# Reordering the first two chunks of a chunked DeltaNet with SwiGLU: copies by pairs of batches, K turned earlier, a chain spread over four gate/value pairs

## The chip, the cores and the metric

The kernel runs on one core of a Trainium2 chip. The metric is device time in microseconds (us). Executions of one kernel on one chip are compared in the same rounds with executions of the kernel before. In the traces PE is TensorE, DVE VectorE, ACT ScalarE and POOL GpSimd. The granted clock is the share of TensorE's full clock that a trace records; "warm" stands for 1.00 and "cold" for 0.50. PSUM is the memory that the matmuls of this kernel write; `ps_pair` gives out two of its banks by a tag.

A ratio is the mean time of one kernel's fast runs over the mean time of the other's fast runs of the same rounds, so it is not quite the ratio of the medians that stand beside it. Below 1 means faster than the kernel before. The interval behind it is a 95% interval.

## The reference, cut to what matters

```python
# q, k, v: (4, 8, 768, 48) float32, beta: (4, 8, 768)
k_n = k / (np.linalg.norm(k, axis=-1, keepdims=True) + 1e-06)
for t in range(S):                                  # S = 768, per batch and head
    y[:, :, t] = np.einsum('bhd,bhde->bhe', q[:, :, t], state)
    v_old = np.einsum('bhde,bhd->bhe', state, kt)
    state = state + bt * np.einsum('bhd,bhe->bhde', kt, vt - v_old)
x = y.transpose(0, 2, 1, 3).reshape(B * S, H * D)   # (3072, 384)
g = x @ w_gate                                      # (384, 1536)
out = (g / (1 + np.exp(-g)) * (x @ w_val)) @ w_out  # (1536, 384)
```

The kernel does this in 12 chunks of 64 time steps. Within a chunk the recurrence becomes products with the inverse of a triangular matrix. VectorE makes these inverses by substitution, for two chunks at a time (a group): the first inverse serves chunks 0 and 1, the second 2 and 3, the third 4 and 5. One chunk then goes through four steps, `p_r`/`p_y` (state times K and Q), `p_u` (inverse times V), `p_s`/`p_y` (new state, output) and `p_f` (transposes of y), and after that through the feed-forward block: six pairs of `p_gate`/`p_val` and two outputs `p_o`, each long enough to keep TensorE full.

## The kernel before

The order of TensorE's work is written out by hand. `point(c)` puts one step of chunk `c`, or one preparation, between two pairs; `prep_step` picks the preparation:

```python
    def prep_step(c):
        if first:
            first.pop(0)()
            return True
        # ... joins of finished inverses ...
        if going:
            next(going.pop())
            return True
        if not q_of or steps("advance", q_of[0] - 1) < 3:
            return False
        k_c, q_c = None, q_of.pop(0)
        if k_of and steps("advance", k_of[0] - AHEAD) >= 4:   # AHEAD = 4
            k_c = k_of.pop(0)
        # ... K of chunk k_c and Q of chunk q_c are turned; an odd k_c also starts an inverse ...
```

The last part of `advance(c)`, the chain of a chunk, with its two copies out of PSUM:

```python
        p_y = recur(ps_pair("p_y", "py"))
        # ...
        p_of_u()
        y = work.tile([128, NB, NJ, 2, D], FP32, name="y", tag="r", bufs=3)
        nc.scalar.copy(y[:, :, :, 0], p_y[:, 0])
        for b in range(2):
            nc.scalar.copy(y[half_of(b), :, :, 1], p_y[half_of(1 - b), 1])
        yield
        p_f = ps_pair("p_f", "py")[:, :, 0 : KT * 128]
        # ... six transposes of y into p_f ...
        nc.scalar.copy(xts[c].rearrange("p t (bp n) -> p t bp n", bp=NB), p_f)
        if c == 0:
            of_state()
        yield
```

And an inverse begins with transposes on VectorE, then a power on GpSimd, then VectorE again:

```python
    def invert(g):
        # ... three transposes into mb (VectorE) ...
        nc.gpsimd.tensor_tensor(out=n, in0=mb[...], in1=half, op=ALU.pow)
        yield WAIT
        nc.vector.tensor_scalar_add(n, n, 1e-6)        # waits for the power
        # ... reciprocal, scaling, 31 substitution steps ...
```

## Time and profile before

| | us |
|---|---|
| median of the three runs that the prediction had | 792.59 (791.41 to 794.15) |
| the execution that was profiled | 788.7, span 786.7, mean granted clock 0.964 |
| TensorE busy | 737.0 of 786.7 |
| TensorE's idle time after 209.5 us | 6.1 |

The prediction shows the lines that bound this kernel. Four more marks of its TensorE timeline serve as a measure (start, length, engine, line, operation, shapes, count): the first `p_o` ends the twelve pairs of chunks 0 and 1, `p_j` is the join of the second inverse, then come chunk 2's `p_u` and its first gate.

```profile
155.44 20.80 PE L754 MATMUL p_o<-wo_sb,h_f 128*128 128x384 f32 x64
182.44 1.92 PE L502 MATMUL p_j<-zt,a_sb 32*32 32x32 f32 x64 [6.20 <-issue]
199.91 1.15 PE L654 MATMUL p_u<-vin,zt 64*64 64x48 f32 x64
209.45 2.86 PE L731 MATMUL p_gate<-x_ffn,wg_sb 128*128 128x256 f32 x12
```

### The profile page before, as it was taken

How to read it: one execution, taken by the hardware profiler on the slowest of the kernel's cores; microseconds unless marked ns; L12 is line 12 of the kernel's file. 1: busy time of each engine (PE TensorE's matmuls, PEld its weight loads, DVE VectorE, ACT ScalarE, POOL GpSimd, SP SyncE). 2: the span in 40 equal slices, each digit the busy share in tenths (PEclk: the TensorE clock that was granted, in tenths of full speed). 3: DMA queues.
4: the chain of work that ended last, by engine and by line, in shares of the span. 5: the costliest groups of instructions: out<-in, count | busy, mean ns of one | idle time of the engine just before them, and what ended most of it. 6: DMA issues, size and time to landing. Idle time of an engine off the chain costs nothing.

```text
span 786.7 us, 21538 instructions
## 1 busy us (share of the span) xinstructions
PE 737.0 (94%) x9800; PEld 588.2 (75%) x9800; DVE 403.8 (51%) x814; ACT 163.6 (21%) x296; POOL 67.9 (9%) x52
## 2 busy tenths in 40 slices
PE   5638899997999999999999999999999999999997
PEld 4537788855788688688688688688688688687784
DVE  5999699994127873067842068832068822021010
ACT  2246243201221211212111112111212111111110
POOL 9106000100003000012000021000020000000000
PEclk9856899998999999999999999999999999999999
DMA  8874244200211200312101112101101000000000
GB/s 149 205 189 116 88 108 137 61 20 12 53 22 23 45 17 3 61 23 42 32 12 19 39 28 43 31 13 23 26 17 22 21 2 2 21 2 1 21 1 20
DMA packets 86683, 34.77 MB, mean 44 GB/s; under 512 B 78848, under 2 KB 81920, under 8 KB 86592
## 3 DMA queue, kind: packets, MB, share of 16 engines
q1 hardware_dynamic: 79872, 27.93, 15.8%
q10 hardware_dynamic: 5952, 5.12, 2.9%
q8 instruction: 77, 1.26, 0.7%
q0 software_dynamic: 768, 0.35, 0.3%
q14 instruction: 14, 0.11, 0.0%
HBM read 28.66 MB, written 4.72 MB: 42 GB/s over the span
## 4 chain that ended last, share of the span: by engine, by line
PE 89%; DVE 5%; ACT 1%; issue 1%; POOL 1%; DMA 1%; ACTq 0%; DVEq 0%
PE p_gate L731 25%; PE p_o L754 24%; PE p_val L731 24%; PE p_g L389 3%; PE p_t L377 2%; PE p_j L517 2%; PE p_u L654 2%; PE p_s L683 2%; PE p_y L671 2%; DVE zb L459 1%; DVE tmp L453 1%; PE p_r L633 1%; PE p_y L642 1%; PE p_f L714 1%; POOL n_t L319 1%
## 5 line engine op out<-in xcount | busy, mean ns | idle before, releaser
L731 PE MATMUL p_gate<-x_ffn,wg_sb 128*128 128x256 f32 x864 | 203.9, 386 | 0.0
L731 PE MATMUL p_val<-x_ffn,wv_sb 128*128 128x256 f32 x864 | 199.3, 381 | 0.0
L754 PE MATMUL p_o<-wo_sb,h_f 128*128 128x384 f32 x576 | 192.4, 491 | 0.0
L731 PEld LDWEIGHTS p_val<-x_ffn,wv_sb 128*128 128x128 f32 x864 | 164.7, 191 | 22.4
L745 DVE TENSOR_TENSOR h_f<-sil,p_val 128x512 f32<-128x512 f32 x72 | 49.3, 685 | 257.1 <-PE p_val L731 256.6
L731 PEld LDWEIGHTS p_gate<-x_ffn,wg_sb 128*128 128x128 f32 x864 | 161.2, 191 | 23.0
L754 PEld LDWEIGHTS p_o<-wo_sb,h_f 128*128 128x128 f32 x576 | 108.7, 192 | 71.8 <-issue 1.4
L740 ACT ACTIVATE sil<-p_gate 128x512 f32<-128x512 f32 x72 | 43.0, 597 | 217.4 <-PE p_gate L731 188.4
L544 POOL TENSOR_TENSOR n_b<-mb,half 128x32 f32<-128x32 f32 x5 | 39.4, 7874 | 441.0 <-DVE mb L423 403.1
L459 DVE TENSOR_TENSOR zb<-zb,tmp 128x31 f32<-128x31 f32 (+15 forms) x186 | 63.7, 343 | 6.4
L453 DVE TENSOR_TENSOR tmp<-zb,mb 128x31 f32<-128x31 f32 (+15 forms) x186 | 63.6, 342 | 5.6
L762 ACT COPY o_sb<-p_o 128x384 f32<-128x384 f32 x24 | 11.5, 478 | 172.0 <-PE p_o L754 165.5
L208 ACT ACTIVATE h_f<-h_f,rebias 128x256 int32<-128x256 uint32 (+2 forms) x36 | 21.0, 612 | 47.0 <-DVE h_f L200 47.0
L692 DVE TENSOR_TENSOR state<-state,p_s 128x768 f32<-128x768 f32 x10 | 9.5, 951 | 26.1 <-PE p_s L683 26.1
L377 PE MATMUL p_t<-ident,kn 128*128 128x128 f32 x96 | 16.8, 324 | 6.5 <-DMA kn<-in_k_dram 5.7
L502 PE MATMUL p_j<-zt,a_sb 32*32 32x32 f32 x256 | 6.2, 214 | 17.3 <-DVE zt L486 11.1
L423 DVE STREAM_TRANSPOSE mb<-a_sb 32x1024 f32<-32x1024 f32 x10 | 21.3, 2135 | 0.3
L377 PEld LDWEIGHTS p_t<-ident,kn 128*128 128x128 f32 x96 | 13.3, 166 | 9.8 <-POOL mask_q L273 4.5
L402 DVE TENSOR_TENSOR p_sb<-p_g,mask_q 128x512 f32<-128x512 f32 x24 | 15.4, 684 | 8.4 <-PE p_g L389 8.4
L389 PEld LDWEIGHTS p_g<-kt 64*64 64x64 f32 x768 | 13.9, 149 | 7.7 <-issue 4.2
L502 PEld LDWEIGHTS p_j<-zt,a_sb 32*32 32x32 f32 x256 | 5.8, 129 | 18.5 <-issue 18.4
L389 PE MATMUL p_g<-kt 64*64 64x64 f32 x768 | 15.5, 236 | 3.7 <-ACT kt L379 2.3
(120 smaller groups left out, 583.9 us busy)
## 6 DMA issues: line engine op xcount, KB each, us to landing
qpad<-in_q_dram SPq DMA_DIRECT2D x48, 96.0 KB, 3.0
vin<-in_v_dram SPq DMA_DIRECT2D x96, 48.0 KB, 2.5
out_dram<-o_sb ACTq DMA_DIRECT2D x48, 96.0 KB, 2.2
kn<-in_k_dram SPq DMA_DIRECT2D x44, 96.0 KB, 3.7
zt<-in_moe_w_out_dram SPq DMA_DIRECT2D x6, 384.0 KB, 3.1
staged<-in_moe_w_out_dram SPq DMA_DIRECT2D x6, 384.0 KB, 3.1
wo_sb<-in_moe_w_gate_dram SPq DMA_DIRECT2D x4, 512.0 KB, 5.5
wo_sb<-in_moe_w_val_dram SPq DMA_DIRECT2D x4, 512.0 KB, 6.9
```

What stands on the lines that cost most here:

```text
L208: nc.scalar.activation(power.bitcast(I32), power, ACTF.Relu, bias=rebias, scale=8.0)
L377: nc.tensor.transpose(p_t[bp][:, at], x[:, bp, 2 * j : 2 * j + 2], ident)
L389: nc.tensor.matmul(p_v[par][half_of(b if of_q else b ^ par), bp, j], kt[c][half_of(par), bp, j, b], xt[half_of(par), bp, j, b],)
L423: nc.vector.transpose(out(rows, 0), in_(rows, 0))
L453: nc.vector.tensor_tensor(out=t_v, in0=zb[:, 0 : j + 1, j : j + 1].to_broadcast([128, j + 1, m]), in1=mb[:, j : j + 1, j + 1 : R].to_broad ...
L459: nc.vector.tensor_tensor(out=zb[:, 0 : j + 1, j + 1 : R], in0=zb[:, 0 : j + 1, j + 1 : R], in1=t_v, op=ALU.add,)
L517: nc.tensor.matmul(p_j[h // n_h][hi, h % n_h, 0:R] if of_d else p_j[h // n_h][hi, h % n_h, R:C], d_t[hi, :, HH * c + h], ident[hi, hi] if ...
L544: nc.gpsimd.tensor_tensor(out=n, in0=mb.rearrange("p j i -> p (j i)")[:, 0 : R * R : R + 1], in1=half, op=ALU.pow,)
L731: nc.tensor.matmul(ps[name][:, i], w_sb[:, t, (f + i) * 128 : (f + i + 1) * 128], xts[c][:, t], start=(t == 0), stop=(t == KT - 1),)
L740: nc.scalar.activation(sil, ps[name], ACTF.Silu)
L745: nc.vector.tensor_tensor(out=hs[c, f], in0=sil, in1=ps["p_val"], op=ALU.mult)
L754: nc.tensor.matmul(p_o, hs[c, f - f % 2][:, f % 2, bp * 128 : (bp + 1) * 128], wo_sb[:, f], start=(f == 0), stop=(f == FT - 1),)
```

## The change

Its intent is to give TensorE work earlier and to fill its waits: shorter copies in chunk 0's chain, so that the first gate starts sooner; chunk 1's chain between four pairs of chunk 0 instead of three; K of chunk 5 in the idle time during chunk 0's outputs. The diff, cut to its core:

```diff
-        nc.scalar.copy(uu, p_u)
+        each = range(NB) if c == 0 else (slice(0, NB),)
+        for bp in each:
+            nc.scalar.copy(uu[:, :, bp], p_u[:, :, bp])
@@ y by pairs of batches; zt and x_ffn likewise
+        for bp in each:
+            nc.scalar.copy(y[:, bp, :, 0], p_y[:, 0, bp])
+            for b in range(2):
+                nc.scalar.copy(y[half_of(b), bp, :, 1], p_y[half_of(1 - b), 1, bp])
@@ prep_step: a K alone may be taken
-        if not q_of or steps("advance", q_of[0] - 1) < 3:
+        k_c, q_c = None, None
+        if q_of and steps("advance", q_of[0] - 1) >= 3:
+            q_c = q_of.pop(0)
+        elif not (hold and k_of and steps("advance", k_of[0] - AHEAD) >= 4):
             return False
-        k_c, q_c = None, q_of.pop(0)
@@ start: K of chunk 1 turned before gram 0, the reciprocal before the transposes
         turned(0, False)
+        turned(1, False, "py")
         gram(0, False)
-        turned(1, False, "py")
+        r_b = first_n()
@@ p_s and the join of chunk 1 go into the first pair
-        next(second)
+        def state_and_join():
+            step("advance", advance, 0)
+            next(second)
-        first.append(second_join)
+        first.extend((state_and_join, second_join, lambda: gram(1, True)))
-        pairs = [(0, 0), (0, 2), (0, 4)] + [(1, 0), (1, 2), (1, 4)]
-        pairs += [(c, f) for f in range(6, FT, 2) for c in range(2)]
+        pairs = [(c, f) for c in range(2) for f in range(0, 8, 2)]
+        pairs += [(c, f) for f in range(8, FT, 2) for c in range(2)]
```

Left out here are the order of the beta loads and of the first transposes of Q, and one `point(2)` fewer ahead of chunk 1's outputs.

More of the change, by code (lines that the diff above doesn't have):

```diff
@@ L336, in load_beta, with first_n @@
         )
-    def first_betas():
+    def first_n():
         n = n_t[0].rearrange("p c h -> p (c h)")
@@ L344, in first_betas @@
         nc.vector.transpose(r_b, r_n)
-        divide_beta(0, r_b)
+        return r_b
     def scale_v_heads(c):
@@ L465, in substitute, with recur @@
             yield
+    def recur(p, m=D):
+        p = p[:, :, 0 : NB * NJ * m]
+        return p.rearrange("p x (bp j d) -> p x bp j d", bp=NB, j=NJ)
     QUADS = [(slice(R * n, R * n + R), R * (n % 2)) for n in range(4)]
@@ L510, in join_late @@
         yield
-        p_j = [p.rearrange("p (h i) -> p h i", i=C) for p in banks("p_j", tags[1])]
-        n_h = HH // 2
+        p_j = recur(ps_pair("p_j", tags[1]), C)
         for of_d in (True, False):
             for h in range(HH):
+                par, bp, j = h // (NB * NJ), h // NJ % NB, h % NJ
                 for s in range(2):
@@ L517, in join_late @@
                     nc.tensor.matmul(
-                        p_j[h // n_h][hi, h % n_h, 0:R] if of_d
-                        else p_j[h // n_h][hi, h % n_h, R:C],
+                        p_j[hi, par, bp, j, 0:R] if of_d else p_j[hi, par, bp, j, R:C],
                         d_t[hi, :, HH * c + h],
@@ L522, in join_late @@
                     )
+        zt_v = zt[:, c].rearrange("p (par bp j) i -> p par bp j i", par=2, bp=NB)
         copies = nc.scalar.copy, nc.vector.tensor_copy if split else nc.scalar.copy
-        for s, copy in enumerate(copies):
-            hi = QUADS[2 * s][0]
-            for n in range(2):
-                copy(zt[hi, c, n * n_h : (n + 1) * n_h], p_j[n][hi])
+        for bp in range(NB):
+            for s, copy in enumerate(copies):
+                hi = QUADS[2 * s][0]
+                copy(
+                    zt_v[hi, :, bp].rearrange("p par j i -> p par (j i)"),
+                    p_j[hi, :, bp].rearrange("p par j i -> p par (j i)"),
+                )
         yield
@@ L616, in join @@
         yield
-    def recur(p):
-        return p[:, :, 0 : NB * NJ * D].rearrange("p x (bp j d) -> p x bp j d", bp=NB, j=NJ)
     def advance(c):
@@ L701, in advance @@
         y = work.tile([128, NB, NJ, 2, D], FP32, name="y", tag="r", bufs=3)
-        nc.scalar.copy(y[:, :, :, 0], p_y[:, 0])
-        for b in range(2):
-            nc.scalar.copy(y[half_of(b), :, :, 1], p_y[half_of(1 - b), 1])
+        for bp in each:
+            nc.scalar.copy(y[:, bp, :, 0], p_y[:, 0, bp])
+            for b in range(2):
+                nc.scalar.copy(y[half_of(b), bp, :, 1], p_y[half_of(1 - b), 1, bp])
         yield
@@ L714, in advance @@
                 nc.tensor.transpose(p_f[:, t, bp], y_f[:, bp, at], ident)
-        nc.scalar.copy(xts[c].rearrange("p t (bp n) -> p t bp n", bp=NB), p_f)
+        x_v = xts[c].rearrange("p t (bp n) -> p t bp n", bp=NB)
+        for bp in each:
+            nc.scalar.copy(x_v[:, :, bp], p_f[:, :, bp])
+        yield
         if c == 0:
             of_state()
-        yield
+            yield
     out_v = out.rearrange("(b s) d -> b s d", s=S)
@@ L907 @@
         norms(0)
-        for at in range(8, 12):
-            load_beta(at)
         nc.vector.memset(places[0][:, 0:1], 0)
         norms(1)
-        for at in range(12, 16):
+        for at in range(8, 16):
             load_beta(at)
@@ L941 @@
         load_v(1)
-        first_betas()
+        divide_beta(0, r_b)
         zb = scale_m(mb, [(slice(0, R), mb)], beta_b[:, 0])
@@ L966 @@
         converts(2)
+        next(first_q)
         next(first_join)
         nc.scalar.copy(mb[:, m_1[0][0]], m_1[0][1])
-        next(first_q)
         step("advance", advance, 0)
@@ L987, in second_join @@
             gens["join", (0,)] = [None, 2]
-            gram(1, True)
-        first.append(second_join)
-        pairs = [(0, 0), (0, 2), (0, 4)] + [(1, 0), (1, 2), (1, 4)]
-        pairs += [(c, f) for f in range(6, FT, 2) for c in range(2)]
+        first.extend((state_and_join, second_join, lambda: gram(1, True)))
+        pairs = [(c, f) for c in range(2) for f in range(0, 8, 2)]
+        pairs += [(c, f) for f in range(8, FT, 2) for c in range(2)]
         for c, f in pairs:
+            early = c == 0 and f < 8
             if c == 1 and f == 0:
@@ L998 @@
             elif f > 0:
-                point(1 if c == 0 and f < 6 else 2)
+                point(1 if early else 2)
             need((6, 12, 18, 18, 24, 24)[f // 2])
-            gate_val(c, f, fill, 1 if c == 0 and f < 6 else None)
+            gate_val(c, f, fill, 1 if early else None)
         need(len(pieces))
@@ L1007 @@
         for bp in range(NB):
-            point(2)
+            if bp > 0:
+                point(2)
             output(1, bp, fill)
```

## The prediction

> **What bounds the kernel now.** I read the page's 40-slice rows first, then busy time by stage, then TensorE's waits, then the timeline of the stages in which TensorE isn't full.
>
> ```profile
> PE   5638899997999999999999999999999999999997
> DVE  5999699994127873067842068832068822021010
> PEclk9856899998999999999999999999999999999999
> ```
>
> From slice 5 on TensorE (PE) is full. Only the first ten slices, 0 to 210 us, can give time back. The same in stages (busy time of each engine, then granted clock, DMA share and GB/s):
>
> ```profile
> 0.00:52.80 52.80, 24.67 (x626) 20.17 (x627) 40.41 (x93) 15.95 (x39) 21.02 (x36) 0.82 0.83 187
> 52.80:72.50 19.70, 15.30 (x454) 13.80 (x454) 19.70 (x64) 11.49 (x22) 7.46 (x1) 0.53 0.38 89
> 72.50:83.30 10.80, 8.58 (x212) 7.71 (x205) 4.26 (x8) 6.44 (x11) 7.08 (x1) 0.76 0.67 189
> 83.30:155.40 72.10, 71.06 (x750) 61.98 (x747) 66.05 (x133) 24.87 (x42) 2.95 (x3) 0.99 0.36 98
> 155.40:176.20 20.80, 20.80 (x65) 11.99 (x64) 19.15 (x51) 0.96 (x2) 0.05 (x1) 1.00 0.08 19
> 176.20:182.50 6.30, 0.10 (x4) 0.09 (x5) 5.82 (x16) 0.00 (x0) 0.00 (x0) 0.85 0.00 0
> 182.50:209.50 27.00, 25.33 (x615) 18.70 (x615) 5.79 (x7) 5.62 (x10) 0.00 (x0) 0.91 0.17 36
> 209.50:786.70 577.20, 571.12 (x7096) 453.72 (x7094) 242.58 (x447) 98.30 (x170) 29.37 (x12) 1.00 0.11 22
> ```
>
> Span less PE busy is PE's idle time: 28.1, 4.4, 2.2, 1.0, 0, 6.2, 1.7 us, and at the end 6.1, mostly the last output's way out. The first 28.1 us lie under VectorE (DVE), which inverts chunk 0's triangle without a gap. The rest by cause:
>
> ```profile
> PE p_j L502 <- DVE zt L486: 11.1, 1, 11.1
> PE p_j L502 <- issue: 6.2, 1, 6.2
> PE p_f L714 <- ACT y L704: 4.8, 3, 1.7
> PE p_g L389 <- ACT zt L527: 2.2, 1, 2.2
> ```
>
> "Issue" for 6.2 us at 176 us is in truth the second inverse: its last transpose ends at 182.34 and p_j starts at 182.44. Chunk 0's chain in the timeline is copies by ScalarE (ACT) between matmuls:
>
> ```profile
> 59.50 2.13 ACT L527 COPY zt<-p_j 32x512 f32<-32x512 f32 x4 [1.83 <-PE p_j L517]
> 63.66 0.80 ACT L663 COPY uu<-p_u 128x768 f32<-128x768 f32 x1 [0.61 <-PE p_u L654]
> 67.03 0.96 ACT L704 COPY y<-p_y 64x384 f32<-64x384 f32 x2
> 69.62 0.80 ACT L715 COPY x_ffn<-p_f 128x768 f32<-128x768 f32 x1 [1.63 <-PE p_f L714]
> 81.38 1.99 PE L389 MATMUL p_g<-qt,kt 64*64 64x64 f32 x64 [2.22 <-ACT zt L527]
> 242.88 6.21 POOL L544 TENSOR_TENSOR n_b<-mb,half 128x32 f32<-128x32 f32 x1 [87.43 <-DVE mb L423]
> ```
>
> **What the Trainium skill says.** "TensorE: Matmul & The Clock Gate", Part 1: the clock is halved after an idle window of about 3.4 us, restored after a busy one, and the windows run free. The trace agrees: 0.50 from 34 to 71.3 us, again from 78.6 to 85 after the 3.8 us of 32x32 matmuls (they run "busy" and still cool it), 180.8 to 187.8, 218.5 to 221.7. "ScalarE: Activation LUTs", What ACT_TABLE_LOAD costs: an ACTIVATE with immediates takes 186 ns plus 0.833 ns per element. Copies here: 478 ns at 384 elements, 797 at 768, which is 0.83 ns per element and 0.16 us fixed, so each split costs about 0.16 us. "GPSIMD Engine Reference", 8. Key points: GpSimd shares its SBUF interfaces with VectorE. The power took 14.55 us beside a full DVE and 6.21 beside a nearly idle one. TensorE's page, Architectural detail: ACT and DVE queues are strictly first in, first out; so a DVE instruction that waits holds all behind it.
>
> **The change part by part.** No work is removed; some copies are split, the rest is order.
>
> 1. Start. K1 is turned before gram 0, and the reciprocal (0.81 us from 23.75 to 24.56) goes ahead of the transposes. But it now waits in DVE's queue for GpSimd's second power. That runs from 12.7 (the beta issues between the two powers are gone) for 3.0 us, to 15.7. Then 0.81 and one 0.69 copy, so the transposes start at 17.2 instead of 16.83 and end at 23.6 instead of 23.22; the betas land at about the same 23.5. The scaling then starts at 24.9, before 25.27. Gain 0.3 us.
>
> 2. Chunk 0's copies by pairs of batches. zt is copied pair by pair, so half of p_u runs during the other half's copies: p_u ends at 63.1 instead of 63.63. uu then waits for the power steps on ACT (to 63.05): two copies of 0.48, to 64.0 instead of 64.46. p_y runs 63.6 to 65.6 instead of 64.5 to 66.5. y is six copies of about 0.32 rather than three of 0.48, behind a mb copy and power steps to 65.5: the last ends at 67.4 instead of 68.0. p_f and x_ffn overlap by halves: x_ffn is ready at 68.75 instead of 70.42. With part 1 gate 0 can start at 68.5. p_s and p_j, 3.1 us ahead of it before, now follow. But the clock is still halved, at about 0.41 us per matmul instead of 0.23, until about 71: gate ends 72.4, p_s and p_j 74.6, where before the same work ended at 75.4. Gain so far 0.8 us.
>
> 3. Four pairs. Value 0 to 77.3, p_j to 81.2, gate 2 cold (3.4 us at half clock costs 1.7) to 85.6, p_g to 86.7, value 2 to 89.3. The 2.2 us wait for zt is filled; allowing for the different order the gain is 3.8 us here. Now a choice of the code: the new condition in the step that picks preparations is already true at the third pair, since chunk 0 has done its steps and the hold is on. So K of chunk 4, not chunk 1's first step, is taken there and its gram within (2.1 us of PE). Chunk 1 gets two steps in the fourth pair, and its last two run back to back ahead of chunk 1's first gate. There PE waits about 1.5 us for the y copies and 0.9 for x_ffn, and 0.7 for vin before p_u; the kernel before had 1.1 in waits there. Gain left: 1.0 us at the end of the twelve pairs. For the same reason K of chunk 5 goes with Q of chunk 2 into chunk 1's pairs, not into chunk 0's outputs. These then end at 155.4 - 1.0 + 2.1 = 156.5, with the 2.1 us saved later on.
>
> 4. The second inverse starts with the end of the pairs. Before, zt's transpose ended 26.9 us after it (155.4 to 182.3), of which some 0.6 was DVE's lag; so 26.3, and p_j starts at 182.8 instead of 182.4. The 20.8 us of outputs do not grow, so PE still idles about 5.5 us and cools.
>
> 5. Gram 5 also starts the third inverse early: behind the second one, in DVE's queue, come its three transposes of 2.1 us and the wait for a 6.2 us power. The transposes end about 8.3 us after p_j starts, the power at 14.5, then scalings and two substitution steps of 3.7 us, then chunk 2's two vin operations of 0.95: p_u can start 20.2 after p_j, where it started 17.5 after. Loss about 3 us.
>
> Sum: +0.4 (p_j) + 3.0 - 2.1 (K5 already done) = +1.3 us, so 793.9 from 792.59.
>
> **Rivals.** *As the words of the change intend*: chunk 1's chain fits the pairs without the 2.4 us hole, and 2.1 us of K5 fill the outputs' wait: -2.4, -2.1 and the 1.0 of the sum without the loss of part 5, and some clock: about 786.5. Against it is my reading of the condition; for it, that somebody wrote it for that. *Clock*: the 32x32 stages of 3.8 us cool PE only if a window falls nearly inside one. Two of three did before. None doing so is worth some 3 us, a third costs 1.7; and a wait of 3 us in part 5 can itself cool it: 797. *DVE as the bound of the pairs*: it was busy 66.1 of 72.1 us. If it can't keep up, the earlier gate gains nothing, p_o waits; but the two pairs' worth of PSUM buffers and the extra PE work (K5) speak against it: at most +1. *K5's transfer*: its load queues behind eight vin loads of 5.9 us and lands about 115 in my times, needed at 116.4; late, it costs 1 or 2 us. *Nothing of part 5*: if the power ends sooner or the fills fall otherwise, its 3 us go: 791.
>
> **Range and chances.** The working says 793.9; the two unsure losses (the cold gate of part 3, the wait of part 5) are each taken in full there. I take off 2.4 us for the chance that they are partial and for the intended reading, and say 791.5, with 786.5 to 796.5 for the rivals. All the idle before 209.5 outside the inverse under part 1 is 15.5 us, and 2% is 15.9; so faster by over 2% is nearly impossible (0.02), within 2% 0.96, slower 0.02.
>
> **What would show it.** First substitution at about 26.3 instead of 26.59; first gate at 68.5 with clock 0.50, not 72.53; K of chunk 4 transposed before chunk 1's p_r, and a hole of some 2.4 us before chunk 1's first gate; no K among chunk 0's outputs; PE's 6.2 us wait at p_j nearly unchanged; p_u of chunk 2 waiting about 3 us for vin, behind a DVE wait on the power. I am wrong if K5 stands in the outputs, if the p_j wait shrinks by over 1.5 us, or if chunk 2's vin is not held back.

## More of the kernel before

A gate is twelve matmuls. At full clock it takes 2.86 us, or 2.75 right behind another product of the block; its length is therefore a clock reading in itself.

## The result, and the profile after

The changed kernel took 797.07 us (median of four, 796.88 to 797.24), the kernel before 793.37 (791.41 to 794.15) in the same rounds: ratio 1.005, interval 1.0029 to 1.0071. That is within 2%, and clearly on the slow side. The predicted 791.5 was too low, and 797.07 lies 0.6 us outside the range.

The profiled execution took 797.02 us with a mean granted clock of 0.949. The clock row of its 40 slices, to be held against the one in the prediction, is lower in slices 1, 2 and 4, and again in slices 6 and 12 (99 to 119 and 219 to 238 us), counted from 1:

```profile
PEclk8555989998989999999999999999999999999999
```

The same marks of the TensorE timeline as above:

```profile
163.31 20.80 PE L764 MATMUL p_o<-wo_sb,h_f 128*128 128x384 f32 x64
190.31 1.92 PE L506 MATMUL p_j<-zt,a_sb 32*32 32x32 f32 x64 [6.19 <-issue]
210.29 1.15 PE L658 MATMUL p_u<-vin,zt 64*64 64x48 f32 x64 [2.21 <-DVE vin L654]
219.99 4.35 PE L741 MATMUL p_gate<-x_ffn,wg_sb 128*128 128x256 f32 x12
230.65 4.15 PE L741 MATMUL p_gate<-x_ffn,wg_sb 128*128 128x256 f32 x12
```

7.9 us are lost by the first `p_o` (163.31 less 155.44). Nothing is added up to `p_j`. Another 2.5 come at `p_u` (19.98 us after `p_j` instead of 17.47), and 2.2 are won back until the end (584.6 us from `p_u` instead of 586.8), in part since K of chunk 5 is done already. The sum is the 8.2 us between the two spans. Where the 7.9 come from, two groups of lines show. First chunk 0's chain; ScalarE's copies:

```profile
65.88 0.32 ACT L709 COPY y<-p_y 128x192 f32<-128x192 f32 x1 [0.41 <-PE p_y L677]
67.19 0.64 ACT L711 COPY y<-p_y 64x192 f32<-64x192 f32 x2
69.46 0.86 ACT L724 COPY x_ffn<-p_f 128x384 f32<-128x384 f32 x2 [1.63 <-PE p_f L721]
```

and TensorE between them:

```profile
67.88 1.54 PE L721 MATMUL p_f<-ident,y 128*128 128x128 f32 x6 [2.07 <-ACT y L711]
```

The first y copy starts only when the last matmul of `p_y` is done, and the first transpose only when the last y copy is done (67.83). In the list of the program's waits just one copy of each group has a wait on TensorE, the first, and `p_f` waits for ScalarE because it is written into the banks that the y copies read:

```
ACT L709 TensorCopy y<-p_y 128x4x48 [waits PE]
ACT L711 TensorCopy y<-p_y 64x4x48 x2
ACT L709 TensorCopy y<-p_y 128x4x48
ACT L711 TensorCopy y<-p_y 64x4x48 x2
PE  L721 Matmult p_f<-ident,y 128x128 [waits PE,Activation]
PE  L721 Matmult p_f<-ident,y 128x128 x5
```

So halving these copies let nothing overlap; it only added fixed cost (six copies in 1.96 us). The first gate starts at 70.37, and runs all 5.49 us at half clock.

Second, the step at chunk 1's first gate. TensorE's timeline, then the engines' busy time in single microseconds (columns: stretch, its length, busy time of PE, PEld, DVE, ACT, POOL with counts, granted clock, DMA share, GB/s):

```profile
113.18 0.96 PE L721 MATMUL p_f<-ident,y 128*128 128x128 f32 x6 [2.33 <-ACT y L711]
115.03 5.49 PE L741 MATMUL p_gate<-x_ffn,wg_sb 128*128 128x256 f32 x12 [0.89 <-ACT x_ffn L724]
```

```profile
112.00:113.00 1.00, 0.00 (x0) 0.00 (x0) 1.00 (x2) 0.98 (x3) 0.00 (x0) 1.00 0.50 86
113.00:114.00 1.00, 0.82 (x6) 0.64 (x6) 0.97 (x3) 0.13 (x1) 0.00 (x0) 0.91 0.21 31
114.00:115.00 1.00, 0.14 (x1) 0.00 (x0) 1.00 (x3) 0.80 (x1) 0.00 (x0) 0.50 0.45 84
119.00:120.00 1.00, 1.00 (x4) 0.78 (x3) 0.00 (x0) 0.00 (x0) 0.00 (x0) 0.50 0.00 0
```

Two waits of 2.33 and 0.89 us stand around 0.96 us of matmuls; together they are called the hole below. The clock halves at about 113.8, before the second wait begins (114.1), and stays so until about 120.7. The gate behind takes 5.49 us instead of 2.86. In the kernel before, `p_f` of chunk 1 and chunk 1's first gate stand apart and do not wait; the longest wait in that chain is 0.71 us.

```profile
101.54 0.87 PE L714 MATMUL p_f<-ident,y 128*128 128x128 f32 x6
104.85 2.75 PE L731 MATMUL p_gate<-x_ffn,wg_sb 128*128 128x256 f32 x12
```

Third, chunk 2's V. VectorE's queue, with GpSimd's power ahead of it:

```profile
198.35 5.44 POOL L551 TENSOR_TENSOR n_b<-mb,half 128x32 f32<-128x32 f32 x1 [35.03 <-DVE mb L423]
203.82 0.90 DVE L558 TENSOR_SCALAR n_b<-n_b 128x32 f32<-128x32 f32 x1 [0.59 <-POOL n_b L551]
209.28 0.95 DVE L654 TENSOR_TENSOR vin<-vin,p_r 128x768 f32<-128x768 f32 x1
```

The third inverse was started early, so its transposes, its wait for the power and its first substitution steps stand in VectorE's queue ahead of chunk 2's `vin`, for which `p_u` waits.

### The profile page after: what moved, and what is told of

Read it like the earlier page. It is cut to its first block, busy times and chain, and to the rows that moved or that the text cites. A ratio compares the mean times of both kernels' runs of the same rounds, so it can differ in the third digit from the quotient of the medians.

```text
span 794.9 us, 21533 instructions
## 1 busy us (share of the span) xinstructions
PE 741.9 (93%) x9800; PEld 590.0 (74%) x9800; DVE 403.7 (51%) x814; ACT 163.9 (21%) x301; POOL 69.6 (9%) x52
## 4 chain that ended last, share of the span: by engine, by line
PE 83%; DVE 11%; POOL 2%; ACT 2%; issue 1%; DMA 1%; ACTq 0%; DVEq 0%
PE p_gate L741 24%; PE p_val L741 23%; PE p_o L764 20%; DVE zb L459 3%; DVE tmp L453 3%; PE p_g L389 2%; PE p_t L377 2%; PE p_u L658 2%; PE p_y L677 1%; PE p_j L521 1%; PE p_s L689 1%; PE p_r L637 1%; PE p_f L721 1%; PE p_y L646 1%; POOL n_t L319 1%
## 5 line engine op out<-in xcount | busy, mean ns | idle before, releaser
L741 PE MATMUL p_gate<-x_ffn,wg_sb 128*128 128x256 f32 x864 | 210.9, 395 | 1.8 <-ACT x_ffn L724 1.8
L741 PEld LDWEIGHTS p_gate<-x_ffn,wg_sb 128*128 128x128 f32 x864 | 164.7, 196 | 26.4 <-ACT x_ffn L724 2.6
L551 POOL TENSOR_TENSOR n_b<-mb,half 128x32 f32<-128x32 f32 x5 | 41.1, 8223 | 373.5 <-DVE mb L423 335.7
L453 DVE TENSOR_TENSOR tmp<-zb,mb 128x31 f32<-128x31 f32 (+15 forms) x186 | 63.5, 342 | 14.8 <-PE p_j L521 9.4
L654 DVE TENSOR_TENSOR vin<-vin,p_r 128x768 f32<-128x768 f32 x11 | 10.5, 954 | 23.9 <-PE p_r L637 23.0
L658 PEld LDWEIGHTS p_u<-vin,zt 64*64 64x64 f32 x768 | 13.4, 141 | 8.3 <-DVE vin L654 3.9
L377 PE MATMUL p_t<-ident,qpad 128*128 128x128 f32 x96 | 14.5, 298 | 4.7 <-DMA qpad<-in_q_dram 4.7
L658 PE MATMUL p_u<-vin,zt 64*64 64x48 f32 x768 | 15.3, 228 | 3.9 <-DVE vin L654 2.9
```

The lines of the kernel that those rows point to most:

```text
L377: nc.tensor.transpose(p_t[bp][:, at], x[:, bp, 2 * j : 2 * j + 2], ident)
L453: nc.vector.tensor_tensor(out=t_v, in0=zb[:, 0 : j + 1, j : j + 1].to_broadcast([128, j + 1, m]), in1=mb[:, j : j + 1, j + 1 : R].to_broad ...
L551: nc.gpsimd.tensor_tensor(out=n, in0=mb.rearrange("p j i -> p (j i)")[:, 0 : R * R : R + 1], in1=half, op=ALU.pow,)
L658: nc.tensor.matmul(p_u[half_of(b), par, bp, j], zt[half_of(b ^ par), par, bp, j], r[half_of(b ^ par), par, bp, j], start=first, stop=True, ...
L741: nc.tensor.matmul(ps[name][:, i], w_sb[:, t, (f + i) * 128 : (f + i + 1) * 128], xts[c][:, t], start=(t == 0), stop=(t == KT - 1),)
```

## The experiments

Fourteen runs (thirteen new kernels, and the changed one again), in batches that shared a chip and the runs of the kernel before, each with five rounds. All outputs are right. My theory after reading the traces: three losses, namely two early K's (hole and cold gate), the early third inverse, and a first gate that cannot start sooner because of PSUM banks and the clock. The rivals: that splitting the copies or the new start is what costs, or that what is saved early is only waited for later.

### Batch 1: which of the orders costs (before: 790.54, 788.88 to 795.26)

**The old rule of picking a preparation**, all else as changed.

```diff
-        elif not (hold and k_of and steps("advance", k_of[0] - AHEAD) >= 4):
+        else:
             return False
```

> The changed kernel with the old rule for picking preparations (no K without a Q). Theory A, the hole: in the changed kernel K of chunk 4 takes a slot of chunk 1's chain, so two of its steps run back to back; TensorE waits 2.33 + 0.89 us there and its clock then halves (first gate of chunk 1 5.49 us instead of 2.86, 2.6 us). Both go: 5.9 us. The third inverse also starts late again, so chunk 2's 2.2 us wait for vin goes: 797.1 - 8.1 = 789.0, that is 4 us under the kernel before. Theory B, the order of the first pair (gate ahead of the state matmuls, on a halved clock) is what costs: only the 2.2 us go, 794.9. The trace should show no gap over 1 us between p_y and the gate of chunk 1, and that gate in 2.9 us, under A.

Measured: 787.13 us, ratio 0.9954 (0.9929 to 0.9979). Chunk 1's chain lies between the pairs, without a wait behind `p_y`:

```profile
103.99 0.82 PE L721 MATMUL p_f<-ident,y 128*128 128x128 f32 x6
107.23 2.75 PE L741 MATMUL p_gate<-x_ffn,wg_sb 128*128 128x256 f32 x12
```

The rest of the change is thus worth about half a per cent, and the new rule alone turns this into a loss. As to the clock behind `p_j`, this execution was an unlucky one: the two `p_o`'s there took 5.42 and 4.28 us.

**K of chunk 5 where the words of the change put it**: the extra K is allowed only once chunk 0's outputs have begun.

```diff
+    outs = []
-        elif not (hold and k_of and ...):
+        elif not (outs and hold and k_of and ...):
@@
         need(len(pieces))
+        outs.append(1)
```

> What the words of the change say: K without a Q is only picked during chunk 0's outputs, so it is K of chunk 5 there. Theory A: the 5.9 us of the hole go as in the run with the old rule, the 2.0 us of K5 lie in TensorE's 6.2 us wait for the second inverse, which falls to about 4.1, and chunk 2's vin still waits about 2.2 us behind the third inverse: 789.2. Theory B: 797.1 - 2.0 = 795.

Measured: 788.54 us, 0.9952 (0.9921 to 0.9984). The wait at `p_j` fell from 6.2 to 4.2 us, as a K among the outputs should make it. But `p_u` of chunk 2 then waited 3.04 us for `vin`, and the clock fell behind it. The gain was eaten.

**The same, with the third inverse held back** until chunk 2 has done its four steps.

```diff
@@ fill_some
-            if fills:
+            if fills and not (fills[0][0] == 2 and steps("advance", 2) < 4):
```

> As the last, but the third inverse is held until chunk 2 has done its four steps. If the 2.2 us wait of chunk 2's p_u comes from the wait on the power in VectorE's queue, it goes: 787.0, 2.2 under the run without the hold. If something else holds vin back, both are the same.

Measured: 783.31 us (781.99 to 784.78), 0.9899 (0.9876 to 0.9923). The wait of `p_u` is gone. Against the run before it, the inverse alone was worth 0.0053 of the ratio, about 4.2 us; 2.2 had been expected.

**The changed kernel with only the inverse held back.**

> The changed kernel with only the third inverse held until chunk 2 is done. If its early start costs what the trace shows, 2.2 us go: 794.9 against 797.1. If the wait is made up for later (the inverse's work then crowds chunk 3), 797.

Measured: 792.25 us, 1.0014 (0.999 to 1.0039). The hole stayed (2.33 and 0.89 us, a gate of 5.14), the wait at `p_u` went. The kernel with the old rule, which has neither the hole nor an early inverse, is 0.0060 below this one, some 4.7 us; its span is 4.6 us shorter (785.2 and 789.8). This is what the early K's cost in time, with their hole and its cold gate.

### Batch 2: the copies, the start and the first pair (before: 790.87, 789.44 to 794.8)

**Chunk 0's copies whole again**: `each = (slice(0, NB),)`, and `zt` by the old halves.

> The changed kernel with only chunk 0's copies whole again. In its trace p_u and p_y gain 0.7 us from the halves (p_y starts 63.85 against 64.51, 0.2 of it from the start), but y costs six copies, 1.96 us instead of 1.46, none of them before p_y's last matmul, and x_ffn two of 0.43 after p_f's last. Theory A, splitting gives at one end what it takes at the other: within 0.3 us of the changed kernel, 797 and a ratio of 1.005 to the kernel before. Theory B, as I had predicted, the halves overlap all along: 1.7 us slower, 798.8, 1.007.

Measured: 796.75 us, 1.0073 (1.0048 to 1.0099). The first gate starts at 69.60 in its trace, within the spread of the kernels with split copies (69.27 to 70.37). Splitting neither helps nor hurts by an amount that these times can show. The ratio is nearest to theory B of the expectation, the median to theory A; the changed kernel did not run in this batch, so the trace has to decide.

**The start undone**: K of chunk 1 and the reciprocal at their old places.

> The changed kernel with only the start as before (gram 0 before K1 is turned, reciprocal after the transposes, beta loads in two lots). Theory: the substitution started 0.17 us earlier in the changed kernel (26.42 against 26.59), so undoing it costs 0.2 us, ratio 1.005. Rival: TensorE's earlier rest in the start sets its clock windows, and the time moves by more than 1 us.

Measured: 796.77 us, 1.0071 (1.005 to 1.0092). No clear effect either: the ratio lies 0.002 above the changed kernel's 1.005 and 1.0053 of other batches, and the intervals overlap. Both rivals of the first kind fall: the loss is in neither.

**`p_s` and `p_j` ahead of the first gate, as before**, on the kernel with K5 in the outputs and the inverse held.

```diff
         second = join_late(0, 1, ("ffn", "py"))
+        step("advance", advance, 0)
+        next(second)
         converts(2)
-        first.extend((state_and_join, second_join, ...))
+        first.extend((second_join, ...))
```

> The kernel with K5 in the outputs and the third inverse held, and the first pair in the order of before: state matmuls and p_j before the first gate. Theory, the cold gate: in every kernel of the new order the first gate ran 4.7 to 5.5 us on the half clock against 2.86 before, after waiting 0.95 us for x_ffn; with p_s and p_j (3.1 us cold) in between, TensorE is busy through that wait and warm by the gate: 1.5 to 2.5 us faster than the kernel without, so about 0.987 of the kernel before instead of 0.990. Rival: the cold time is only moved to other matmuls, p_g waits for zt again: no gain, 0.990.

Measured: 784.86 us, 0.9926 (0.9903 to 0.9949). I had expected it to be faster than the kernel it was built on, and it was not (783.31, 0.9899, in the batch before). The gate itself was warm, 2.86 us at 71.40. But chunk 1's chain was then early against VectorE: its `p_u` waited 2.85 us for `vin`, and the clock fell there instead (a gate of 4.01 us). The rival held here: time was moved, not saved.

**Useless matmuls in chunk 0's two waits**, on the same kernel: four in the wait for y and two in the wait for `x_ffn`, into a spare PSUM tile (each shows as two in the trace).

```diff
+        if c == 0:
+            warm(4, "px")       # n times: matmul(p[:, 0, 0:128], ident, x[:, 0:128])
         yield
         y_f = y.rearrange(...)
@@
+        if c == 0:
+            warm(2, "px")
         x_v = xts[c]...
```

> The same kernel in the new order, with four matmuls whose result nobody reads in TensorE's 2.07 us wait for y and two in its 0.95 us wait for x_ffn. They do no useful work; the only thing they can change is the clock. Theory, the cold gate: TensorE is then busy from 63.7 us on, its clock doubles before the gate or early in it: the gate in 2.9 to 3.8 us instead of 4.7 to 5.5, and 1.5 us faster, 0.988 of the kernel before. Rival, the clock follows the kind of matmul or the memory traffic: no change or slower by what the extra matmuls overrun.

Measured: 782.56 us (778.49 to 784.44), 0.9882 (0.9855 to 0.9909). The median is 0.75 us lower than without them, from another batch, which the times don't settle. The traces show the step itself; without them (first fence) and with them (second):

```profile
69.42 4.68 PE L741 MATMUL p_gate<-x_ffn,wg_sb 128*128 128x256 f32 x12 [0.95 <-ACT x_ffn L724]
75.11 1.20 PE L506 MATMUL p_j<-zt,a_sb 32*32 32x32 f32 x64
```

```profile
69.80 2.86 PE L751 MATMUL p_gate<-x_ffn,wg_sb 128*128 128x256 f32 x12 [0.50 <-ACT x_ffn L728]
73.67 1.20 PE L506 MATMUL p_j<-zt,a_sb 32*32 32x32 f32 x64
```

The gate starts 0.4 later and still lets `p_j` start 1.4 earlier, since the clock is at 1.00 by then.

### Batch 3: the hole by itself, and the banks (before: 790.84, 787.91 to 794.49)

**Useless matmuls in the hole**: the changed kernel with eight and three of them in chunk 1's two waits.

> The changed kernel with eight matmuls that nobody reads in TensorE's wait for chunk 1's y (2.33 us) and three in the wait for its x_ffn (0.89 us). The two waits stay, only the clock can change. Theory: of the 5.9 us that the hole cost, 3.2 are the waits and 2.6 the halved clock in the gate behind it; the gate falls from 5.1 to 5.5 us to 2.9, and the ratio to the kernel before falls by 0.3%, from 1.005 to 1.002. Rival: the clock falls for another reason (the small matmuls ahead of it), the gate stays at 5 us and the time is the changed kernel's.

Measured: 795.06 us (794.02 to 796.42), 1.005 (1.0016 to 1.0083). Its trace:

```profile
112.07 0.87 PE L723 MATMUL p_f<-ident,y 128*128 128x128 f32 x6 [0.36 <-ACT y L711]
113.83 2.86 PE L750 MATMUL p_gate<-x_ffn,wg_sb 128*128 128x256 f32 x12 [0.22 <-ACT x_ffn L728]
```

```profile
114.00:115.00 1.00, 1.00 (x5) 0.89 (x6) 0.74 (x2) 0.00 (x0) 0.00 (x0) 1.00 0.80 142
```

The times do not show a gain: expected was a ratio of 1.002, and 1.005 is the changed kernel's own. The trace shows one that is lost again further on. The clock stays at 1.00 and the gate takes 2.86 us instead of 5.49. It ends 3.8 us sooner than in the changed kernel's first trace; 1.1 of these were there ahead of the hole already (`p_y` at 108.62 instead of 109.73), so 2.7 are the clock's in this pair of traces, since the waits for y and `x_ffn` are still as long, only filled. At `p_j` 3.9 us are won (186.37 instead of 190.31). Then over a third is given back: `p_u` of chunk 2 waits 2.80 instead of 2.21, the `p_o` behind it takes 4.54 instead of 2.85, and chunk 2's first gate is only 2.2 us sooner (217.79). How much the clock takes varies: with the hole left open, the gate behind it took 5.49, 5.14, 5.49, 5.15 and 4.24 us in five traces, which is 1.4 to 2.6 more than 2.86. This batch alone could not say how much of it the times keep, so two more runs were made (batch 4).

**`p_f` of chunk 0 in other banks**, on the kernel with K5 in the outputs and the inverse held.

```diff
-        p_f = ps_pair("p_f", "py")[...]
+        p_f = ps_pair("p_f", "px" if c == 0 else "py")[...]
```

> The kernel with K5 in the outputs and the third inverse held, with chunk 0's p_f in p_u's PSUM banks instead of p_y's. Theory: the copies by pairs could not overlap p_f because p_f is in the banks that the last y copy still reads; in other banks the first half of p_f starts after three of six y copies, p_f ends 0.8 us earlier and the gate starts 0.8 us earlier (68.6 where it was 69.4), 0.1% in the time. Rival: p_f waits for the whole of y anyway: its start is unchanged at 0.04 us after the last y copy.

Measured: 783.77 us, 0.9904 (0.9875 to 0.9934), no faster. In its trace

```profile
65.16 1.90 PE L721 MATMUL p_f<-ident,y 128*128 128x128 f32 x6 [1.09 <-ACT y L711]
68.01 5.49 PE L741 MATMUL p_gate<-x_ffn,wg_sb 128*128 128x256 f32 x12 [0.95 <-ACT x_ffn L724]
```

the wait for y is 1.09 us instead of 2.07, and the gate starts 1.4 us earlier than in the fence above. So the shared banks did hold `p_f` back. But the gate is now all at half clock and ends only 0.6 us earlier (73.4 and 74.0): of the 1.4 us of the earlier start, less than half is left in these two traces.

**Useless matmuls in chunk 0's waits and in the wait at `p_j`** (eight of 256 columns there), same base.

> The kernel with the idle matmuls in chunk 0's y and x_ffn waits (0.988 of the kernel before), and eight more of 256 columns, 3.8 us, in the 4.2 us wait for the second inverse. Theory: p_j then runs 1.2 us and the outputs behind it 2.85 instead of 1.92 and 4.2: 2 us, ratio 0.986. Rival: the small p_j matmuls cool it anyway, no change.

Measured: 779.14 us (778.7 to 784.3), 0.9868 (0.9832 to 0.9905). With the wait at `p_j` filled, that join takes 1.20 us instead of 1.92 and the `p_o` behind it 2.85 instead of 4.22. But the second `p_o` behind it now takes 4.14 us instead of 2.85, so that `p_u` follows `p_j` after 16.5 us instead of 17.3: of the 2.1 us saved at the join, 0.8 are kept. The times do not tell this kernel from the one without the filled join (0.9882, another batch).

**All together**: K5 in the outputs, inverse held, other banks, useless matmuls in the three waits (three instead of four in the wait for y).

> All of it together: K5 in the outputs, the third inverse held, p_f in other banks, idle matmuls in the waits of chunk 0 and of the second inverse. If the parts add up: 0.985 of the kernel before, 779; if they share one gain (the first gate's clock), 0.987.

Measured: 778.52 us (777.07 to 784.43), 0.9854 (0.9817 to 0.9892), the best version of all; it beats both kernels, the one before by 1.5%. Beside the kernel with only the other banks, in the same batch, its median is 5.3 us lower; the two intervals overlap a little. With the waits filled, the banks now show their worth in the trace: the gate starts at 68.69 and is warm. Times do not tell this kernel from the one before it.

```profile
68.69 2.86 PE L750 MATMUL p_gate<-x_ffn,wg_sb 128*128 128x256 f32 x12 [0.23 <-ACT x_ffn L728]
```

### Batch 4: do the two losses hide each other? (before: 791.27, 788.55 to 793.9)

**The changed kernel again**, unaltered.

> The changed kernel itself, again, so that it stands beside the next run on the same chip in the same rounds. Its ratio to the kernel before was 1.005 with four runs, and 1.0073 and 1.0071 for two variants that should hardly differ from it. Expected: 1.005 to 1.008. If it is about 1.007, then filling the hole in chunk 1 (795.06 us, 1.005 in another batch) was worth some 2 us in the times too, as in its trace; if it is 1.005 or lower, it was worth nothing.

Measured: 796.24 us (793.96 to 797.42), 1.0053 (1.0037 to 1.007). The result repeats in another batch. The profile fell on its fastest execution, 793.96 us, and is worth reading beside the first one:

```profile
188.65 1.92 PE L506 MATMUL p_j<-zt,a_sb 32*32 32x32 f32 x64 [6.20 <-issue]
208.84 1.15 PE L658 MATMUL p_u<-vin,zt 64*64 64x48 f32 x64
```

Here `p_u` shows no wait at all, and yet it starts 20.2 us after `p_j`, where it did so 20.0 after it in the first trace with a wait of 2.21. In this execution the `p_o`'s between ran slowly (5.49 and 4.43 us) and took up the time. Chunk 2's `vin` is done 19.9 us after the start of `p_j` in both traces (here at 208.55), and 14.8 after it in the kernel before: this shows the early inverse. The distance of `p_u` alone does not, since slow `p_o`'s make the same one. The kernel with the old rule, whose third inverse is late and whose `vin` is done 17.4 us after `p_j`, has it too, 20.0 us:

```profile
179.65 1.92 PE L506 MATMUL p_j<-zt,a_sb 32*32 32x32 f32 x64 [6.20 <-issue]
199.63 1.15 PE L658 MATMUL p_u<-vin,zt 64*64 64x48 f32 x64
```

So in the repeat's profiled execution the early inverse cost nothing that the clock had not taken already. For the hole, the expectation had said that a ratio of 1.005 or lower here would mean that filling it alone was worth nothing in the times (1.005 there). 1.0053 is that, within the noise.

**Both losses treated**: useless matmuls in the hole, and the third inverse held.

> The changed kernel with both losses treated where they lie: useless matmuls in the two waits of chunk 1's hole, so that its gate runs at full clock, and the third inverse held back until chunk 2 has made its four steps. With the hole filled alone, the trace showed 3.9 us gained up to the join behind the outputs, and 2 us of it given back where chunk 2's p_u waited 2.8 us for vin instead of 2.2 and the clock fell once more. Theory (two separate losses, of which the second hides part of the first): with the inverse held, all of the 3.9 us remain and the 2.8 us of the inverse come on top, so 6 to 7 us less than the changed kernel: about 790 us, ratio 0.998 to 1.000. Rival (what is saved ahead of the outputs is always given back later): no more than the inverse held alone showed, 792, ratio 1.0014.

Measured: 789.15 us (788.11 to 794.83), 0.9993 (0.9963 to 1.0023). The ratio is 0.0060 below that of the changed kernel beside it, about 4.7 us, and the medians lie 7.1 apart, because two of the six runs took over 794 us. `p_u` follows `p_j` after 17.2 us again. Expected were 6 to 7 us less than the changed kernel and a ratio of 0.998 to 1.000; the ratio met it. The rival's 1.0014 is still inside the interval, so the times alone do not exclude it. The traces speak against it: `p_j` at 186.23, as with the hole filled alone, and `p_u` 3.0 us sooner than there, both savings present. That the clock behind the hole costs time is thus shown in the traces; in the times it is not separated from noise (0.9993 here, and 1.0014 with only the inverse held, in another batch).

## Why the prediction was wrong

The order of things was read rightly; what failed was the size of one term, part 3, and a deduction that had no trace behind it.

- **What the new rule picks**: as said. K of chunk 4 at the third pair, K of chunk 5 in chunk 1's pairs, no K among the outputs, the last two steps of chunk 1 back to back.
- **Part 1**: the substitution started at 26.42 instead of 26.59; said was 26.3.
- **Part 2**, "x_ffn is ready at 68.75 instead of 70.42" and a first gate at 68.5: it started at 70.37, and at 69.3 to 69.8 in eight other traces that leave chunk 0's chain up to there as it is, the repeat's among them. I let half of the copies overlap with the matmuls. The traces showed that none of y's or `x_ffn`'s did. The banks' share of this was shown by moving `p_f`. That copies out of a tile in PSUM begin only after its last matmul was read from the program's waits, not tested.
- **Part 3**, "Gain left: 1.0 us at the end of the twelve pairs": this is the step that failed. Said was a first `p_o` 1.1 us later than before; it came 7.9 later. Of the 6.8 us between, the late `x_ffn` makes 1.9, the first gate 1.6 (5.49 instead of 3.9), the hole 0.8 (3.2 instead of 2.4), and the gate behind the hole 2.6, which I had at full clock. The second gate of chunk 0 gave 1.6 back, since it was warm. These sum to 5.3. A further 0.5 is a wait that my sum lacked: the gram of chunk 4 waits for ScalarE's copy of kt (at 95.44, and in every trace with the early K). The other 1.0 us I can't name. In the repeat the first `p_o` came at 161.64, so 5.1 later than said; the gate behind the hole took 4.24 us there, and the second gate of chunk 0 was cold, as said. Nor do the terms shown give the 1.0: 3.8 less the growth of the waits, 3.1 against 1.1, is 1.8, and the working does not say what took the other 0.8. The mechanism of the hole was right, its clock was not in the sum: I had named a wait that cools TensorE as a risk for part 5, and not for the 2.4 us that I had put there myself. The traces with useless matmuls show it: with the same waits filled, the clock stays up, and the way from chunk 1's last `p_y` to the first `p_o` takes 50.7 us in both, against 52.1 to 53.6 in the five traces with the hole open.
- **Part 4**: the wait at `p_j` was 6.19 us, nearly unchanged as said, if not the 5.5 of the working. It starts 27.0 us after the first `p_o`, as before, not 26.3.
- **Part 5**, "Loss about 3 us", with `p_u` "20.2 after p_j": it was 20.0 and 20.2 in the two traces; in the second the slow `p_o`'s set it, so that match is luck. Holding the inverse back was worth 0.0036 to 0.0053 of the ratio, 2.8 to 4.2 us. So its size was about right.
- **K5 already done, 2.1 us back**: from `p_u` to the end, 2.2 in the first trace and 3.7 in the repeat (583.1 us instead of 586.8). The near match is luck in part. The trace of the kernel before has a wait of 1.57 us there, for y at 332.42, which the changed kernel's has not, and in the first trace chunk 2's first gate took 4.35 us instead of 2.86.
- **The deduction**: the working said 793.9, and I took 2.4 us off for partial losses and for the intended reading. The reading was certain enough from the code. Of the two losses that I called unsure, the wait of part 5 came in full; the cold second gate came in the repeat (4.54 us) and not in the first trace (2.86), where the larger losses above stood in its place. Without the deduction 797.07 would still have been above the value, but inside a range as wide.
- **The base**: the trace that I read was of a 788.7 us execution, while I added its differences to a median of 792.59. Between the two profiled executions lie 8.2 us, between the medians 3.7. So more than half of what separates the traces is that the kernel before was caught in a fast execution; no slower one of it was profiled. The kernel before varies more from one execution to the next than most of the terms that I summed.

As to rivals in the prediction: of the clock I wrote 797 with "a wait of 3 us in part 5 can itself cool it". That the number was nearly right is luck: most of the clock's loss was at the first gate and in the hole of part 3. Behind part 5 chunk 2's first gate ran slowly in the first trace (4.35 us) and not in the repeat (2.86).

Two readings in it were loose: GpSimd's power of 14.55 us stood beside a VectorE that was busy for 11.7 of them, not full, and ten slices end at 197 us, not at 210.

What stays open: 1.0 us of the twelve pairs, what the slower executions of the kernel before lose, and which of the 32x32 stages cools TensorE in a given execution.

## What to carry to other kernels

When a change brings two dependent steps together, price the wait between them twice: once as idle time and once as the half clock of what follows, which here cost 1.4 to 2.6 us behind 3.2 of waiting, by five traces. Work started early on an engine with a queue in order delays whatever is queued behind it; look at when that queued work is done, since a cold stretch of TensorE can hide the wait, and can make the same delay by itself. And a split copy let the next product start sooner here only when that product had banks of its own; whether its source, too, must come free by halves was not tested.

## What the Trainium skill lacked or had wrong

- "TensorE: Matmul & The Clock Gate", Part 1 gives the rule as no idle gaps above about 3.4 us. Here a gap of 2.33 us with part of six transposes (`p_f`) behind it was enough: the clock halved at about 113.8, before the second gap of 0.89 us, and stayed so for 6.8 us (a gate of 5.49 us instead of 2.86). Filling both gaps kept it at 1.00. The page does say elsewhere that short idle stretches between groups of matmuls can do this, and that transposes do not count as busy in the same way; no run here separates the two. How much activity a window needs is what it lacks.
- "Perfetto Trace Analysis", Optimizing Tensor Performance, Matmuls says that independent groups should rotate through PSUM banks so that the copies of one overlap the matmuls of the next. The run with `p_f` in other banks fits this, with halves of one group (1.09 us of waiting instead of 2.07). That passage lacks that cutting the copies into halves does not do the same in one pair of banks: `p_f` still waited for the last of six copies, 2.07 us where three whole copies had made it wait 1.57.
